# Ten instead of thirteen weight blocks converted in the first stage of an attention and feed-forward kernel, and the 1e-9 of the softmax sums kept beside them

## Chip, cores and metric

The kernel runs on one core of a Trainium2 chip. The metric is the device time of one execution in microseconds, the median of several runs.

## What is computed

Windowed attention (4 batches, 8 heads, 576 positions, head size 64; each position sees itself and the 63 before it), and behind it two feed-forward parts over all 2304 tokens. q, k and v are 32-bit floats; the weights are 64-bit floats, which arrive as pairs of 32-bit words.

```python
scores = scale * q @ k.T;  scores = where(0 <= i - j < 64, scores, -1e9)
attn = exp(scores - max);  attn = attn / (sum(attn) + 1e-9)
x = (attn @ v)                                   # 2304 x 512
x = ((x @ w1) * (x @ w2)) @ w3 @ w_out           # 512 -> 1024 -> 1024 -> 512
h = x @ w_in;  out = (h * sigmoid(h)) @ w_out2   # 512 -> 2048 -> 512
```

## The kernel before

**Stages.** Stage W (`phase_w`, 16 steps s of two parts) multiplies w3 and w_out into one matrix w' (eight blocks `wp`), so that the first feed-forward part needs one product less. Six blocks of 384 tokens then pass through `phase_a`: 16 units of 12 matmuls (L510) form a = x w1 and b = x w2 for eight slices f, their product p (L518), and eight more units multiply p by w' and store x2. The last stage (from L665) does the second feed-forward part. Attention is woven through stage W and the first five passes of `phase_a`.

**Attention.** There are 72 groups g (128 queries of one pair of heads), each with an even and an odd half, 2g and 2g + 1, in `half`. The even half has on PE the scores s of g, the output o of g - 2 and the transposes t of g - 1; on DVE the masked scores with their row minimum (L276); on ACT the copy of the transposes (L315 for the first 17, "plain" groups) and the exponentials, which write their row sums by accum_out (L287). The odd half has `normalise` on DVE (L295 adds 1e-9 to the sums, L297 takes the reciprocal, L299 multiplies), ACT's copy of o to xr (L339), and for g + 2 from group 17 on `prep_qk`: ACT rounds q and k to qkhi (L241), POOL (klo, L245) and DVE (L248) form what rounding left. Then SP loads q and k of up to g + 4; a load waits until its buffer (two of them) has been read. The first 17 groups load q to a tile of its own, qp. Half 28 + n goes out ahead of unit n of the first projection, so that o and t of two groups stand between each second pair of units.

**Conversions.** A weight block (128 x 512 values, 512 KB) passes through a line of 40 blocks and four closing steps; the counter t in `steps_to` is the step. At step t SP loads block t if `loads_to` has not done so, DVE does block t - 1's fraction and sign (`stage1`: L125, L128) and POOL adds (L132); for the 16 blocks of w1 and w2, ACT then forms the rounded part of block t - 3 (L140) and DVE or POOL the remainder of block t - 4, the low half (L144): DVE if t is even, POOL if it is odd. Last, ACT begins block t (`stage0`: L114, L115; both wait for its load).

**What sets the order.** The order on each engine is the order in which the code is written. `W12_BY` says how many of the 16 blocks of w1 and w2 (numbered here 0 to 15 in the order of their use: 0 to 3 in unit 0, 4 to 7 in unit 1, 8 to 11 in unit 8, 12 to 15 in unit 9) stand in the line by each s. `ready[s]` is the number of steps by which s has its data. In stage W each s runs to `ready[s + 2]` and loads three blocks further:

```python
loads_to(ready[s + 2] + (3 if s > 1 else 0))
steps_to(first + (ready[s + 2] - first) * (part + 1) // 2, (nc.vector, nc.gpsimd), 3)
```

The last `ready` is W12_B + 24 (L444). What is left of the line goes with the units of the first projection (the hook in L552).

Of the kernel before, what the change touches and what calls it, by code (L numbers as in the profile page):

```python
# [9 lines left out]
F32 = mybir.dt.float32  # L10
# [3 lines left out]
AF = mybir.ActivationFunctionType  # L14
ALU = mybir.AluOpType
# [12 lines left out]
MASKED = -8.0e9  # L28
PLAIN = 17
CVB, CVR = 5, 3  # L30
W12_A, W12_B = 3, 13
W12_BY = [n * W12_A // 8 for n in range(8)] + [W12_A + n * (W12_B - W12_A) // 8 for n in range(8)]


# [8 lines left out]
def tile_window_attention_ffn(ctx, tc, qkv, vp, mask, ident, w1, w2, w3t, w_out, w_in, w_out2, out):  # L43
# [7 lines left out]
    nc = tc.nc  # L51
# [4 lines left out]
    att = late.enter_context(tc.tile_pool(name="att", bufs=2, side="right"))  # L56
    psa = late.enter_context(tc.tile_pool(name="psa", bufs=1, space=PSUM))

    def f32(ap):
        return ap.bitcast(F32)  # L60
# [7 lines left out]
    def slot(name, tag, dims, dtype=F32, pool=None, bufs=1):  # L68

        t = (pool or main).tile([128, SLOTS.get(tag, 1024)], dtype, name=name, tag=tag, bufs=bufs)  # L70
        n = int(np.prod(dims))
        letters = "abcd"[: len(dims)]
        sizes = {x: d for x, d in zip(letters[1:], dims[1:])}
        return t[:, :n].rearrange(f"p ({' '.join(letters)}) -> p {' '.join(letters)}", **sizes)

    def split(hi, lo, src, eng_hi, eng_lo):

        if eng_hi == "act":
            nc.scalar.copy(out=hi, in_=src)  # L79
        else:  # L80
            (nc.vector if eng_hi == "dve" else nc.gpsimd).tensor_copy(hi, src)
        (nc.vector if eng_lo == "dve" else nc.gpsimd).tensor_tensor(  # L82
            out=lo, in0=src, in1=f32(hi), op=ALU.subtract
        )
# [4 lines left out]
    def accumulator(name, shape):  # L89

        turn[0] = (turn[0] + 1) % converting["banks"]
        return ps.tile(shape, F32, name=name, tag=f"ps{turn[0]}")
# [59 lines left out]
    def loads_to(n):  # L152
        while done["load"] < min(n, len(line)):
            if line[done["load"]]:
                line[done["load"]].load()
            done["load"] += 1
# [3 lines left out]
    def fill(n=1):  # L160

        for _ in range(min(n, len(parts))):
            parts.pop(0)()

    def steps_to(n, lo=(nc.vector,), keep=0):

        while done["step"] < min(n, len(line)):
            t = done["step"]
            loads_to(t + 1)
            fill(len(parts))  # L170
            if t >= 1 and line[t - 1]:
                parts.extend(line[t - 1].stage1())
            fill(len(parts) - keep)
            if t >= 4 and line[t - 4]:
                line[t - 4].low_part(lo[t % len(lo)])
            if t >= 3 and line[t - 3]:
                line[t - 3].high_part()
            if line[t]:
                line[t].stage0()
            done["step"] += 1  # L180
# [9 lines left out]
    qk_raw, v_raw, qk_st, v_st, s_st, p_st = {}, {}, {}, {}, {}, {}  # L190
# [3 lines left out]
    k_lo = [att.tile([128, 384], F32R, name=f"klo{i}", tag=f"klo{i}", bufs=1) for i in range(2)]  # L194
    k_p = [att.tile([128, 384], F32, name=f"kp{i}", tag=f"kp{i}", bufs=1) for i in range(2)]
    v_p = [att.tile([128, 320], F32, name=f"vp{i}", tag=f"vp{i}", bufs=1) for i in range(3)]
    HEADS = (0, slice(0, 64)), (1, slice(64, 128))
    xhl = {}
    loaded = set()
# [2 lines left out]
    def plain(g):  # L202


        return g < PLAIN

    def place(g):
        blk, r = divmod(g, 3 * NPAIR)
        return blk * 3 + r % 3, r // 3

    def load_qk(g):
        if g < NG and g not in loaded:
            loaded.add(g)
            u, c = place(g)
            if not plain(g):
                qk_raw[g] = att.tile([128, 768], F32, name=f"qk{g}", tag="qk", bufs=2)
                nc.sync.dma_start(out=qk_raw[g], in_=qkv[u, c, :, 0:768])
                return
            qk_raw[g] = att.tile([128, 128], F32, name=f"qp{g}", tag="qp", bufs=2)
            nc.sync.dma_start(out=qk_raw[g], in_=qkv[u, c, :, 0:128])  # L220

            for h, hs in HEADS:
                n = slice(384 + h * 192, 576 + h * 192)
                nc.sync.dma_start(out=k_p[g % 2][hs, h * 192 : h * 192 + 192], in_=qkv[u, c, hs, n])
# [11 lines left out]
    def prep_qk(g):  # L236
# [5 lines left out]
        q, k = slice(128, 384), slice(384, 768)  # L242
        for h, hs in HEADS:
            n = slice(384 + h * 192, 576 + h * 192)
# [38 lines left out]
    def exps(g):  # L283
        nm, rs = s_st[g]
        for h in range(2):
            x = sm[g % 2][:, h, :]
            nc.scalar.activation(  # L287
                out=x, in_=x, func=AF.Exp, scale=-1.0, bias=nm[:, h : h + 1], accum_out=rs[:, h : h + 1]
            )

    def normalise(g):
        _, rs = s_st.pop(g)
        x = sm[g % 2]
        fill()
        nc.vector.tensor_scalar_add(rs, rs, 1.0e-9)  # L295
        fill()
        nc.vector.reciprocal(out=rs, in_=rs)  # L297
        fill()
        nc.vector.tensor_tensor(out=x, in0=x, in1=rs.unsqueeze(2).to_broadcast([128, 2, 192]), op=ALU.mult)  # L299
# [12 lines left out]
    def split_t(g, t_ps):  # L312
# [6 lines left out]
        nc.scalar.copy(out=b[:, :, 0, :], in_=own)  # L319
        for h, hs in HEADS:  # L320
            nc.scalar.copy(out=a[hs, h, 0], in_=before[hs])
        nc.vector.tensor_tensor(out=b[:, :, 1, :], in0=own, in1=f32(b[:, :, 0, :]), op=ALU.subtract)
        for h, hs in HEADS:
            nc.vector.tensor_tensor(out=a[hs, h, 1], in0=before[hs], in1=f32(a[hs, h, 0]), op=ALU.subtract)
# [68 lines left out]
    def halves_to(n):  # L393
        while halves[0] < min(n, LAST_HALF):
            half(halves[0])
            halves[0] += 1
# [10 lines left out]
    def phase_w():  # L407
# [38 lines left out]
        for t in k_p + [f32(t) for t in k_lo]:  # L446
            for h, hs in HEADS:
                nc.gpsimd.memset(t[hs, 192 - h * 192 : 384 - h * 192], 0.0)
# [43 lines left out]
    def phase_a(blk, hooks):  # L492
        x = xhl[blk]
        p = [slot(f"p{blk}", "p", [5, 2, NB], F32R), slot(f"q{blk}", "q", [3, 2, NB], F32R)]
        p = [p[f // 5][:, f % 5] for f in range(8)]
        a_sb = None

        def unit(n):
            halves_to(W_HALVES + 24 * blk + n + 1)
            hooks(n)  # L500

        for s in range(16):
            f, m = divmod(s, 2)
            unit(s)
            fs = slice((f % 4) * 128, (f % 4 + 1) * 128)
            acc = accumulator(f"ab{blk}_{s}", [128, NB])
            for k in range(4):
                w = weights["12", (2 * m + f // 4) * 4 + k]
                for n, (l, r) in enumerate(PASSES):
                    nc.tensor.matmul(  # L510
                        acc, lhsT=w[:, l, fs], rhs=x[k // 2][:, k % 2, r, :],
                        start=(k == 0 and n == 0), stop=(k == 3 and n == 2),
                    )
            if m == 0:
                a_sb = slot(f"a{blk}_{f}", "st", [2, NB], bufs=4)
                nc.scalar.copy(out=a_sb[:, 0], in_=acc)
            else:
                nc.vector.tensor_tensor(out=a_sb[:, 1], in0=acc, in1=a_sb[:, 0], op=ALU.mult)  # L518
                split(p[f][:, 0], p[f][:, 1], a_sb[:, 1], "act", "pool")
        for o in range(4):  # L520
            acc = accumulator(f"x2_{blk}_{o}", [128, NB])
            for f in range(8):
                if f % 4 == 0:
                    unit(16 + 2 * o + f // 4)
                    if blk + 1 < NBLK and o == 3 and f == 0:
                        split_x(blk + 1, 3)
                    if blk + 1 < NBLK and o < 3 and f == 4:
                        split_x(blk + 1, o)
                for n, (l, r) in enumerate(PASSES):
                    nc.tensor.matmul(  # L530
                        acc, lhsT=wp[f][:, l, o * 128 : (o + 1) * 128], rhs=p[f][:, r, :],
                        start=(f == 0 and n == 0), stop=(f == 7 and n == 2),
                    )
            x2 = slot(f"x2s{blk}_{o}", "st", [NB], bufs=4)
            nc.scalar.copy(out=x2, in_=acc)
            nc.scalar.dma_start(out=x2d[o, :, blk * NB : (blk + 1) * NB], in_=x2)

    def new_pt():
# [5 lines left out]
        for i in range(2):  # L544
            for h, hs in HEADS:
                nc.gpsimd.memset(f32(pt[i, 0][hs, 1 - h]), 0.0)

    with tc.manual_schedule():
        xr = slot("xr", "xr", [4, NB])
        phase_w()  # L550
        new_pt()
        phase_a(0, lambda n: steps_to(W12_B + 24 + (n + 1) * (20 - W12_B) // 6, (nc.vector, nc.gpsimd)))  # L552
        for blk in range(1, NBLK - 1):
            phase_a(blk, lambda n: None)
        late.close()
# [33 lines left out]
        for first, last in ((0, 3), (3, 7), (7, 11), (11, 16)):  # L589
# [6 lines left out]
            for key, src in chunks:  # L596
                tag = tags.pop(0)
# [68 lines left out]
        for i in range(1, len(jobs) + 1):  # L666
            if i < len(jobs):
                j, f = jobs[i]
# [93 lines left out]
```

## Time and profile before

| what | value |
|---|---|
| median of 3 runs | 869.71 us (869.51 to 870.24) |
| profiled execution | 868.85 us, span 867.1 us |
| PE busy | 847.3 us (98% of the span) |
| DVE, ACT, POOL busy | 452.3, 497.8, 445.6 us |
| granted PE clock | 1.00 over the span |
| chain that ended last | PE 86%, DVE 1%, ACT 1% |

Busy time is the time in which the engine works on an instruction; PE's is modelled from pipelined matmuls. A timeline names, for a wait, the instruction of another engine that ended it last. t16 below means the three transposes of group 16 on PE, o15 the output of group 15, qkhi17 the rounding of group 17, klo17 its remainder on POOL.

### The profile page before, as it was taken

What the parts mean: (1) busy time and instruction counts of PE and PEld (TensorE: products, weight loads), DVE (VectorE), ACT (ScalarE), POOL (GpSimd) and SP (SyncE); (2) the same over time, 40 slices, a digit from 0 to 9 for tenths busy, and PEclk for the clock granted to TensorE, in tenths of its full rate; (3) what the DMA queues carried; (4) which work ended last, traced back from release to release, by engine and by line L of the source; (5) the groups of instructions that cost most, each with busy time, mean ns of one, the idle gap of its engine ahead of it and who ended that gap; (6) DMA issues with size and microseconds to landing.
All of it is one profiled execution on the core that took longest, in us unless ns stands there. A gap on an engine that the chain in (4) does not pass through costs nothing.

```text
span 867.1 us, 13353 instructions
## 1 busy us (share of the span) xinstructions
PE 847.3 (98%) x4362; PEld 737.0 (85%) x4362; DVE 452.3 (52%) x1158; ACT 497.8 (57%) x1243; POOL 445.6 (51%) x494
## 2 busy tenths in 40 slices
PE   5999999999999999999999999999999999999998
PEld 2444799999999999999998888888888888888896
DVE  5989878778778778676465884111111111111111
ACT  6888868788788788786666774222222222222222
POOL 4768566666666666665685886223322232223222
PEclk9999999999999999999999999999999999999999
DMA  8998233323333333330687200200020002000100
GB/s 296 336 291 261 95 97 108 120 92 101 120 92 110 112 95 120 118 92 33 245 319 274 82 1 0 98 1 1 0 98 1 1 0 73 2 1 0 49 1 25
DMA packets 43204, 85.83 MB, mean 99 GB/s; under 512 B 4864, under 2 KB 22528, under 8 KB 43136
## 3 DMA queue, kind: packets, MB, share of 16 engines
q1 hardware_dynamic: 37088, 75.55, 26.8%
q10 hardware_dynamic: 6048, 9.44, 3.0%
q8 instruction: 35, 0.57, 0.3%
q14 instruction: 33, 0.27, 0.1%
HBM read 75.53 MB, written 9.44 MB: 98 GB/s over the span
## 4 chain that ended last, share of the span: by engine, by line
PE 86%; DVE 1%; ACT 1%; issue 0%; POOLq 0%; POOL 0%; ACTq 0%; DVEq 0%
PE h L633 23%; PE o L652 23%; PE ab L510 22%; PE x L530 12%; PE t L309 2%; PE o L343 2%; PE s L266 1%; PE s L270 1%; PE o L344 1%; ACT sm L287 0%; DVE rs L295 0%; DVE a L518 0%; ACT p L79 0%; DVE cv_b L128 0%; POOLq L758 0%
## 5 line engine op out<-in xcount | busy, mean ns | idle before, releaser
L82 POOL TENSOR_TENSOR g<-sg,g 128x512 fp32r<-128x512 f32 (+1 forms) x80 | 94.9, 1186 | 249.6 <-ACT g L79 235.1
L633 PE MATMUL h<-x2t,hl 128*128 128x512 f32 (+1 forms) x960 | 213.4, 371 | 0.0
L652 PE MATMUL o<-hl,g 128*128 128x512 f32 x864 | 211.2, 391 | 0.1
L639 DVE TENSOR_TENSOR sg<-h,sg 128x512 f32<-128x512 f32 (+1 forms) x80 | 51.1, 638 | 288.2 <-ACT sg L638 288.2
L633 PEld LDWEIGHTS h<-x2t,hl 128*128 128x128 f32 x960 | 169.4, 188 | 33.9
L652 PEld LDWEIGHTS o<-hl,g 128*128 128x128 f32 x864 | 160.9, 188 | 35.6 <-POOL g L82 0.5
L638 ACT ACTIVATE sg<-h 128x512 f32<-128x512 f32 (+1 forms) x80 | 44.4, 555 | 195.4 <-PE h L633 195.4
L510 PE MATMUL ab<-xa,hl 128*128 128x384 f32 x576 | 119.2, 341 | 0.0
L510 PE MATMUL ab<-xb,hl 128*128 128x384 f32 x576 | 115.4, 334 | 0.0
L510 PEld LDWEIGHTS ab<-xb,hl 128*128 128x128 f32 x576 | 101.3, 188 | 0.0
L510 PEld LDWEIGHTS ab<-xa,hl 128*128 128x128 f32 x576 | 99.2, 188 | 0.0
L132 POOL TENSOR_TENSOR cv_b<-cv_b,cv_r 128x512 int32<-128x512 int32 x48 | 73.5, 1531 | 20.9 <-DVE cv_b L128 10.0
L79 ACT CAST g<-sg 128x512 fp32r<-128x512 f32 (+1 forms) x80 | 46.3, 578 | 63.2 <-DVE sg L639 62.3
L353 POOL TENSOR_TENSOR xr<-ot 128x128 f32<-128x128 f32 x55 | 31.5, 573 | 97.6 <-DVE ot L352 61.4
L245 POOL TENSOR_TENSOR klo<-qk,qkhi 64x192 fp32r<-64x192 f32 x110 | 66.7, 607 | 8.3 <-PE ab L510 2.0
L530 PE MATMUL x<-p,wp 128*128 128x384 f32 x360 | 68.2, 340 | 0.0
L287 ACT ACTIVATE sm<-sm,nm 128x192 f32<-128x192 f32 x144 | 64.4, 449 | 4.4 <-DVE nm L276 3.1
L530 PEld LDWEIGHTS x<-p,wp 128*128 128x128 f32 x360 | 61.9, 188 | 0.1
L125 DVE TENSOR_SCALAR cv_z<-cv_b 128x512 int32<-128x512 int32 x72 | 49.4, 687 | 15.5 <-ACT cv_b L114 14.6
L114 ACT ACTIVATE cv_b<-words 128x512 f32<-128x512 f32 x72 | 48.2, 670 | 9.7 <-DMA words<-in_w_out 5.2
L128 DVE SCALAR_TENSOR_TENSOR cv_b<-words,cv_z 128x512 int32<-128x512 int32 x72 | 49.4, 686 | 3.2
L115 ACT ACTIVATE cv_r<-words 128x512 int32<-128x512 uint32 x72 | 47.6, 661 | 0.0
(80 smaller groups left out, 1254.6 us busy)
## 6 DMA issues: line engine op xcount, KB each, us to landing
qk<-in_qkv SPq DMA_DIRECT2D x55, 384.0 KB, 3.2
words<-in_w_out SPq DMA_DIRECT2D x24, 512.0 KB, 8.3
words<-in_w3t SPq DMA_DIRECT2D x16, 512.0 KB, 6.0
words<-in_w SPq DMA_DIRECT2D x16, 512.0 KB, 6.4
words<-in_w_in SPq DMA_DIRECT2D x16, 512.0 KB, 7.2
v<-in_qkv SPq DMA_DIRECT2D x55, 96.0 KB, 2.7
x2d<-x2s ACTq DMA_DIRECT2D x24, 192.0 KB, 1.9
out_x<-osb ACTq DMA_DIRECT2D x18, 256.0 KB, 2.1
```

The costliest lines, as they stand in the source:

```text
L82: (nc.vector if eng_lo == "dve" else nc.gpsimd).tensor_tensor(out=lo, in0=src, in1=f32(hi), op=ALU.subtract)
L114: nc.scalar.activation(out=f32(self.b), in_=f32(self.high), func=AF.Copy, scale=2.0**-112)
L125: nc.vector.tensor_scalar(out=self.z, in0=b, scalar1=3, scalar2=None, op0=ALU.logical_shift_left)
L128: nc.vector.scalar_tensor_tensor(out=b, in0=self.high, scalar=-0x80000000, in1=self.z, op0=ALU.bitwise_and, op1=ALU.bitwise_or)
L132: nc.gpsimd.tensor_tensor(out=x, in0=b, in1=self.r, op=ALU.add)
L245: nc.gpsimd.tensor_tensor(out=k_lo[g % 2][hs, h * 192 : h * 192 + 192], in0=t[hs, n], in1=f32(hi[hs, n]), op=ALU.subtract)
L287: nc.scalar.activation(out=x, in_=x, func=AF.Exp, scale=-1.0, bias=nm[:, h : h + 1], accum_out=rs[:, h : h + 1])
L510: nc.tensor.matmul(acc, lhsT=w[:, l, fs], rhs=x[k // 2][:, k % 2, r, :], start=(k == 0 and n == 0), stop=(k == 3 and n == 2),)
L530: nc.tensor.matmul(acc, lhsT=wp[f][:, l, o * 128 : (o + 1) * 128], rhs=p[f][:, r, :], start=(f == 0 and n == 0), stop=(f == 7 and n == 2),)
L633: nc.tensor.matmul(acc, lhsT=weights["in", f // 4, k][:, l, fs], rhs=x[:, k, r, :], start=(k == 0 and i == 0), stop=(k == 3 and i == 2),)
L639: nc.vector.tensor_tensor(out=sg, in0=acc, in1=sg, op=ALU.mult)
L652: nc.tensor.matmul(oacc[t], lhsT=g[:, l, t * 128 : (t + 1) * 128], rhs=weights["out", f][:, r, :], start=(f == 0 and i == 0), stop=(f == 1 ...
```

## The change

Three things are edited. First, `W12_B` goes from 13 to 10, so that stage W ends 34 steps into the line instead of 37 and `W12_BY` spreads seven blocks over its second half instead of ten; the hook of the first projection then runs two steps in unit 0 and one in each of units 1 to 8, where it ran one in each of units 0 to 4 and two in unit 5. Second, the exponentials write their sums into tiles of [128, 2, 2] whose second column was set to 1e-9 once, and the addition of 1e-9 becomes a reduction over the two columns. Third, q of the plain groups is loaded into the tag of qkhi instead of one of its own.

```diff
-W12_A, W12_B = 3, 13
+W12_A, W12_B = 3, 10
...
+    sums_of = [att.tile([128, 2, 2], F32, name=f"es{i}", tag=f"es{i}", bufs=1) for i in range(2)]
+    for t in sums_of:
+        nc.vector.memset(t, 1.0e-9)
...
-            qk_raw[g] = att.tile([128, 128], F32, name=f"qp{g}", tag="qp", bufs=2)
+            qk_raw[g] = att.tile([128, 768], F32, name=f"qp{g}", tag="qkhi", bufs=2)[:, 0:128]
...
-                out=x, in_=x, func=AF.Exp, scale=-1.0, bias=nm[:, h : h + 1], accum_out=rs[:, h : h + 1]
+                out=x, in_=x, func=AF.Exp, scale=-1.0, bias=nm[:, h : h + 1], accum_out=sums_of[g % 2][:, h, 0:1]
...
-        nc.vector.tensor_scalar_add(rs, rs, 1.0e-9)
+        nc.vector.tensor_reduce(out=rs, in_=sums_of[g % 2], axis=mybir.AxisListType.X, op=ALU.add)
...
-        phase_a(0, lambda n: steps_to(W12_B + 24 + (n + 1) * (20 - W12_B) // 6, (nc.vector, nc.gpsimd)))
+        phase_a(0, lambda n: steps_to(W12_B + 26 + n, (nc.vector, nc.gpsimd)))
```

Lines of the changed file are three higher than those of the kernel before from L200 on. SP's loads from the end of stage W into the first projection, before (the last two loads of words are blocks 14 and 15; qk17 and those after it are the groups with a rounded q and k):

```order
L107 DMA words_898<-in_w2 128x1024
L107 DMA words_900<-in_w2 128x1024
L220 DMA qp15_944<-in_qkv 128x128
L224 DMA kp1_77<-in_qkv 64x192 x2
L230 DMA vp2_80<-in_vp 128x320
L220 DMA qp16_1025<-in_qkv 128x128
L224 DMA kp0_76<-in_qkv 64x192 x2
L217 DMA qk17_1029<-in_qkv 128x768
L217 DMA qk18_1031<-in_qkv 128x768
L230 DMA vp0_78<-in_vp 128x320
L217 DMA qk19_1113<-in_qkv 128x768
```

and in the changed kernel (words_1054, 1094 and 1140 are blocks 13, 14 and 15; block 12's load is the last that stage W issues):

```order
L233 DMA vp2_80<-in_vp 128x320
L223 DMA qp16_1001<-in_qkv 128x128
L227 DMA kp0_76<-in_qkv 64x192 x2
L220 DMA qk17_1005<-in_qkv 128x768
L220 DMA qk18_1007<-in_qkv 128x768
L233 DMA vp0_78<-in_vp 128x320
L107 DMA words_1054<-in_w2 128x1024
L220 DMA qk19_1091<-in_qkv 128x768
L233 DMA vp1_79<-in_vp 128x320
L107 DMA words_1094<-in_w2 128x1024
L107 DMA words_1140<-in_w2 128x1024
```

Three loads of words that stood in stage W now stand in the first projection, one ahead of qk19 and two behind it and the vp after it.

ACT from group 17's rounding in unit 3 to the exponentials of group 16 and the rounded part after them, before:

```order
L241 CAST qkhi17_1108<-qk17_1029 128x768
L140 CAST hl_1121<-cv_b_1002 128x512
L79 CAST p0_977<-a0_1_1102 128x384
L315 COPY pw1_87<-t15_1149 128x320
L287 ACTIVATE sm0_72,rs16_1142<-sm0_72,nm16_1141 128x192 x2
L140 CAST hl_1157<-cv_b_1041 128x512
```

and in the changed kernel:

```order
L244 CAST qkhi17_1086<-qk17_1005 128x768
L140 CAST hl_1101<-cv_b_978 128x512
L114 ACTIVATE cv_b_1103<-words_1094 128x512
L115 ACTIVATE cv_r_1104<-words_1094 128x512
L79 CAST p0_944<-a0_1_1080 128x384
L318 COPY pw1_91<-t15_1133 128x320
L290 ACTIVATE sm0_72,es0_81<-sm0_72,nm16_1125 128x192 x2
L140 CAST hl_1147<-cv_b_1017 128x512
```

Two instructions that read block 14's words (words_1094) now stand between the rounded part of a block and the cast of p, ahead of the exponentials of group 16; block 15's (words_1140) stand behind them.

DVE from the sums of group 14 to the product L518 (L521 in the changed file) of unit 1, before (behind one pair of L125 and L128):

```order
L295 TENSOR_SCALAR rs14_982<-rs14_982 128x2
L297 RECIPROCAL rs14_982<-rs14_982 128x2
L299 TENSOR_TENSOR sm0_72<-sm0_72,rs14_982 128x384
L125 TENSOR_SCALAR cv_z_1034<-cv_b_1002 128x512
L128 SCALAR_TENSOR_TENSOR cv_b_1002<-words_847,cv_z_1034 128x512
L144 TENSOR_TENSOR hl_1000<-cv_b_879,hl_1000 128x512
```

and in the changed kernel, from the first pair after the masked scores of group 14:

```order
L125 TENSOR_SCALAR cv_z_963<-cv_b_900 128x512
L128 SCALAR_TENSOR_TENSOR cv_b_900<-words_789,cv_z_963 128x512
L144 TENSOR_TENSOR hl_898<-cv_b_804,hl_898 128x512
L125 TENSOR_SCALAR cv_z_972<-cv_b_968 128x512
L128 SCALAR_TENSOR_TENSOR cv_b_968<-words_823,cv_z_972 128x512
L298 TENSOR_REDUCE rs14_949<-es0_81 128x2
L300 RECIPROCAL rs14_949<-rs14_949 128x2
L302 TENSOR_TENSOR sm0_72<-sm0_72,rs14_949 128x384
L125 TENSOR_SCALAR cv_z_1010<-cv_b_978 128x512
L128 SCALAR_TENSOR_TENSOR cv_b_978<-words_825,cv_z_1010 128x512
```

A low half (hl_898, block 7) and a second pair now stand ahead of the sums of group 14.

## Rows read from the trace of the kernel before

**Rows 1.** The table by stretches of the span: length, busy time (and instructions) by engine, PE clock, DMA.

```profile
57.00:97.50 40.50, 37.26 (x136) 20.14 (x135) 37.62 (x82) 33.49 (x80) 32.17 (x28) 1.00 0.72 225
...
126.00:402.00 276.00, 276.00 (x1730) 275.36 (x1729) 214.16 (x717) 225.80 (x680) 174.21 (x262) 1.00 0.34 104
```

**Rows 2.** Timeline of PE, behind 57 us: start us, us, engine, line, operation [idle before <-releaser].

```profile
64.03 0.49 PE L336 MATMUL o<-pw,vp 128*128 128x128 f32 x2 [1.59 <-ACT xr L339]
...
81.90 0.49 PE L336 MATMUL o<-pw,vp 128*128 128x128 f32 x2 [0.80 <-ACT xr L339]
...
83.50 0.52 PE L309 MATMUL t<-id_sb,sm 128*128 128x128 f32 x3 [0.72 <-DVE sm L299]
...
101.85 0.81 PE L262 MATMUL s<-kp,qp 128*128 128x384 f32 x2
...
115.26 0.52 PE L309 MATMUL t<-id_sb,sm 128*128 128x128 f32 x3 [0.68 <-DVE sm L299]
...
120.82 0.50 PE L309 MATMUL t<-id_sb,sm 128*128 128x128 f32 x3
```

**Rows 3.** Timeline of DVE in the second half of stage W.

```profile
59.43 0.69 DVE L125 TENSOR_SCALAR cv_z<-cv_b 128x512 int32<-128x512 int32 x1
...
60.82 0.35 DVE L276 CUSTOM_DVE_ANT_0 sm<-s,mask_sb 128x192 f32<-128x192 f32 x1
...
85.21 1.49 DVE L144 TENSOR_TENSOR hl<-cv_b,hl 128x512 fp32r<-128x512 f32 x1
```

**Rows 4.** Lines 295, 297 and 299 by source: duration in ns, min/median/max.

```profile
L295 DVE TENSOR_SCALAR rs<-rs x72: 152/432/1140, 13.8 to 402.7; 128x2 f32<-128x2 f32 x72
L297 DVE RECIPROCAL rs<-rs x72: 150/166/168, 14.6 to 403.0; 128x2 f32<-128x2 f32 x72
L299 DVE TENSOR_TENSOR sm<-sm,rs x72: 557/558/1549, 14.8 to 403.2; 128x384 f32<-128x384 f32 x72
```

**Rows 5.** Timeline of DVE in the first projection.

```profile
102.62 0.68 DVE L144 TENSOR_TENSOR hl<-cv_b,hl 128x512 fp32r<-128x512 f32 x1
103.22 0.55 DVE L518 TENSOR_TENSOR a<-ab,a 128x384 f32<-128x384 f32 x1
...
113.19 1.14 DVE L295 TENSOR_SCALAR rs<-rs 128x2 f32<-128x2 f32 x1 [1.24 <-ACT sm L287]
...
119.54 0.56 DVE L299 TENSOR_TENSOR sm<-sm,rs 128x384 f32<-128x384 f32 x1
```

**Rows 6.** Timeline of POOL in the first projection.

```profile
108.54 1.46 POOL L245 TENSOR_TENSOR klo<-qk,qkhi 64x192 fp32r<-64x192 f32 x2
...
113.01 1.29 POOL L144 TENSOR_TENSOR hl<-cv_b,hl 128x512 fp32r<-128x512 f32 x1
```

**Rows 7.** Timeline of ACT in the first projection.

```profile
99.58 0.67 ACT L114 ACTIVATE cv_b<-words 128x512 f32<-128x512 f32 x1
...
100.72 0.46 ACT L516 COPY a<-ab 128x384 f32<-128x384 f32 x1
...
107.58 0.84 ACT L241 CAST qkhi<-qk 128x768 fp32r<-128x768 f32 x1
...
111.43 0.51 ACT L79 CAST p<-a 128x384 fp32r<-128x384 f32 x1 [2.48 <-DVE a L518]
```

**Rows 8.** Timeline of SP: the loads that it issues.

```profile
99.60 0.38 SPq L230 DMA_DIRECT2D vp<-in_vp  x1
110.02 0.33 SPq L217 DMA_DIRECT2D qk<-in_qkv  x1
110.44 0.38 SPq L230 DMA_DIRECT2D vp<-in_vp  x1
```

**Rows 9.** DMA issues at 83.3 us, in the whole span, at 110.0 us: xcount, KB, us to landing.

```profile
words<-in_w SPq DMA_DIRECT2D x1, 512.0 KB, 4.7
...
words<-in_w SPq DMA_DIRECT2D x16, 512.0 KB, 6.4
...
qk<-in_qkv SPq DMA_DIRECT2D x1, 384.0 KB, 3.0
```


## Prediction before the run

> **What bounds the kernel now.** I read the table by stretches first, because the share of PE over the span hides the stages. In [rows 1] the reader is to see two regimes: in the second half of stage W (57 to 97.5 us) DVE is busy 37.62 of 40.50 us and PE 37.26, so either can be late; from 126 to 402 us PE is busy for all of 276 us. All that the change moves lies before 126 us, so a microsecond lost or won there moves the end by as much.
>
> Next the waits of PE, in its timeline [rows 2]. Behind 57 us four are left: 1.59 and 0.80 us for ACT's copy of an attention output, 0.72 us and (in the first projection, at t16) 0.68 us for DVE's product L299. What comes late behind the first is in DVE's timeline [rows 3]: a second conversion pair, from L125 at 59.43 on, stands ahead of the mask-and-minimum L276 at 60.82, whose result the exponentials wait for.
>
> **1. Three conversions leave stage W.** The order shows it does what it says: one step fewer at s = 8, 11 and 14. At s = 8 the pair of [rows 3] goes, so L276 starts 60.82 - 59.43 = 1.39 us earlier, and with it all that led to the 1.59 us. The 0.80 and 0.72 us come behind s = 11, which loses a step too. All three together are 3.11 us. Against it: the low halves take DVE and POOL by the parity of the step, and the new numbering gives blocks 3 to 6 to DVE, which POOL did before. One on DVE takes up to 1.49 us [rows 3], of which less than half is its own. DVE loses 3 x 1.4 us of conversions in a stretch with 2.9 us of slack, so the cover mostly holds; I leave 0.5 us of stalls and take **-2.6 us**. Ends: -3.1 (all three gone) and -1.4 (only the wait that the removed pair explains).
>
> **2. The sums beside 1e-9.** L295 goes from a one-input tensor_scalar to a reduce of 2 x 2 elements; the nearest rows price it at 0.15 to 0.17 us (the shortest L295, and L297) [rows 4], so its own cost is nothing. What it can give is its waiting: 0.432 us is its median and 1.140 its longest. At 113.19 it takes 1.14 us [rows 5], and POOL's 1.29 us operation from 113.01 ends at 114.30 [rows 6], when L295 ends too: DVE stood behind POOL. L297 never does (150 to 168 ns), L299 does (up to 1549 ns) [rows 4]. So the wait either goes, 0.98 us at t16, or is met two instructions later. I take 0.5 us, inside term 4. The Trainium skill, "SBUF — State Buffer", section "Who interferes with whom", says that VectorE and GpSimd take turns on one port pair, whole instructions at a time; that a tensor_scalar can take it, a tensor_reduce on trn2 never, and that a tensor_tensor with both inputs in SBUF is held by a GpSimd read as well. By that rule, which the rows bear out, L299 inherits the wait and the edit is worth 0 here instead of 0.98; the sum would be 0.5 us higher.
>
> The two memsets of four elements run before any data has come, at some 0.17 us each. The tile that q now shares with qkhi makes ACT's conversion of group 17 wait for the scores of group 15, which PE starts at 101.85 [rows 2], over five microseconds before ACT gets there; both are nothing.
>
> **3. The first projection starts with more to do.** Unit 0 now holds two steps instead of one, and block 7's low half. On DVE that is a pair of 1.4 us and a low half of 0.68 us [rows 5] ahead of the product of unit 1, L518, which ran at 103.22 and now comes 2.1 us later, at 105.3. PE needs block 7's low half last in unit 1, which ended at 101.85 [rows 2]; on DVE two pairs, a low half and the normalisation, 4.3 us, lie between it and L518, so it is there by 101.0. ACT converts p behind L518 and had no gap from there to qkhi17 at 107.58 [rows 7], so the 2.1 us are carried: qkhi17, some 0.8 us long, ends at about 108.4 + 2.1 = 110.5. What PE loses to this at t14 and t15 is part of the next term.
>
> **4. Blocks 13, 14 and 15 are loaded late.** The loads are issued up to line 37 ahead in stage W; before, 37 + 3 = 40 was all of them, now 34 + 3 = 37. The last three are issued by SP inside units 2, 3 and 4, each just before the step that converts it. Block 13's follows the vp load issued at 99.60 [rows 8] and is needed at about 108: hidden even by 6.4 us of landing. Block 14's stands on SP behind the load of qk19, and that waits until POOL's klo17 has read the buffer. In the profile klo17 began at 108.54 for 1.46 us [rows 6], and SP issued qk19 at 110.02, vp at 110.44 [rows 8]. On ACT, block 14's first conversion follows qkhi17 and one high half directly: ACT is in order, so everything behind it waits, above all the exponentials of group 16.
>
> Price: klo17 done at 110.0 + 2.1 = 112.1; two issues, 0.9 us, so the load leaves at 113.0. Landing: a 512 KB block in a thin stream took 4.7 us, the median of the 16 is 6.4, and 384 KB alone took 3.0 [rows 9]. I take 4.7, the nearest (a small vp ahead of it there too): 117.7. ACT's pair takes 100.72 - 99.58 = 1.14 us [rows 7]: done at 118.85. There the split of p starts, which started at 111.43 before: 7.4 us later. From it to t16 it took 115.26 - 111.43 = 3.8 us, now 0.5 less. So t16 comes at 122.2: **+6.9 us**, all of it on PE, since t16 was already late by 0.68. Ends: landing in 3.0 us and L299 not held, +4.7; landing in 6.4 and L299 held, +9.1. The Trainium skill, "DMA: Bandwidth & Descriptors", section "Anatomy of one DMA", fits 2.0 us plus bytes at 436 GB/s (on the GpSimd path), an estimate of 3.2 us for a block; the rows here are above it by 1.5 us and more, and by it the sum would be 1.5 us lower.
>
> **5. The two groups behind it.** From L299 of t16 (ended 115.1) to that of t17 (119.54 + 0.56 = 120.1, [rows 5]) the chain over ACT and DVE took 5.0 us, and PE 120.82 - 115.26 = 5.56 between its own [rows 2]. Now block 15's pair stands on ACT ahead of qkhi18 (+1.1), DVE gets there sooner by most of the 0.5 us that L299 gained (+0.4), and block 15's L125 and L128 stand on DVE behind qkhi18 (+1.4): 7.9 against 5.56, **+2.3 us** (0.9, the DVE pair alone, to 2.6). One group later two high halves and a low half are extra: **+0.5 us** (0 to 1.2), the same for the low half of block 15, which unit 9 needs. Then ACT and DVE are back to the old load, and PE bounds.
>
> **Sum:** -2.6 + 6.9 + 2.3 + 0.5 = **+7.1 us**. The profiled execution took 868.85 us (span 867.1), which makes 875.95; the median of the runs lies 0.86 above it, so I forecast **876.8 us**. By the ends the forecast's own case runs from 869.7 - 3.1 + 4.7 + 0.9 + 0 = 872.2 to 869.7 - 1.4 + 9.1 + 2.6 + 1.2 = 881.2.
>
> **Rivals.**
> - *The late load is hidden, and the kernel gets faster.* Place: ACT's wait for block 14 in unit 3. It decides at about 111 us, when ACT gets there: if the block is in by then, ACT has 2.48 us of idle time behind it [rows 7] for the moved work, terms 4 and 5 vanish, and the 0.68 us of t16 go with stage W's 2.6: 869.7 - 3.3 = 866.4. For it: PE waits for none of these conversions themselves. Against it: SP would have to issue the load some five microseconds sooner, and the order puts it behind qk19. Chance 0.07.
> - *Gain and loss cancel.* The block lands in 3.0 us, L299 is not held (+4.7), all three waits of stage W go (-3.1), and the groups behind need nothing: 869.7 + 1.6 = 871.3. For it: the DMA queue is nearly empty there. Against it: three favourable ends at once. Chance 0.10.
> - *Stage W gives nothing.* DVE becomes its bound: four low halves at 1.49 us instead of 0.68 are 3.2 us, about what the conversions free. The time is then 869.7 + 9.7 = 879.4. For it: DVE's 93% in [rows 1]. Against it: POOL has fewer operations to be in the way. Chance 0.13.
>
> **How the numbers follow.** The forecast has 0.70, with 876.8 as its time. A measurement of this kernel tells about 0.2%, 1.7 us, from no change. Faster by more than that is the first rival, 0.07; within it the second and the forecast's low edge, 0.11; slower the rest, 0.82. The range leaves out the first rival and the far ends: 871.0 to 880.8.
>
> **What would show it.** Right: in the changed profile SP issues two loads of words just behind qk19; ACT idles some 5 to 7 us for DMA before a cast of words in unit 3; PE waits 6 to 8 us for ACT or DVE at half 34 (o15, t16), and 1 to 3 us at t17; the 1.59 us of stage W is gone. Wrong: ACT's wait for that block is under 2 us, or PE runs on through t16; then the first rival holds. If the waits of PE in stage W are as before, the third does. L295's successor should never take more than 0.2 us, and L299 should be longer than before where L295 waited.

## The result, and the profile after

| what | before | after |
|---|---|---|
| median of the runs | 869.65 us (869.51 to 870.24, 4 runs) | 878.94 us (877.77 to 880.48, 4 runs) |
| profiled execution | 868.85 us, span 867.1 us | 878.86 us, span 877.1 us |

The ratio is 1.0106, with a 95% interval from 1.0092 to 1.012: the change makes the kernel 9.3 us slower. 876.8 us was forecast, with a range of 871.0 to 880.8.

The table by stretches of the span, as in [rows 1], with the columns named there (us, PE, PEld, DVE, ACT, POOL, PE clock, DMA share, GB/s), after and then before:

```profile
57.00:97.50 40.50, 40.20 (x153) 23.12 (x152) 35.76 (x86) 31.84 (x81) 25.15 (x22) 1.00 0.65 202
97.50:126.00 28.50, 18.39 (x101) 16.90 (x100) 18.39 (x41) 15.68 (x38) 17.28 (x15) 0.85 0.34 112
126.00:140.00 14.00, 14.00 (x85) 14.00 (x85) 10.01 (x32) 10.80 (x35) 9.98 (x12) 0.94 0.31 102
```

```profile
97.50:126.00 28.50, 27.82 (x175) 27.18 (x173) 22.65 (x59) 21.25 (x59) 19.08 (x19) 1.00 0.30 94
```

In the second half of stage W PE rose from 37.26 to 40.20 of 40.50 us: the waits there are gone. Between 97.5 and 126 us, the first projection, PE has 18.39 us instead of 27.82, and for the first time the granted clock is below 1: 0.85 there, 0.94 up to 140 us. Its timeline (start us, us, engine, line, operation, [idle before <-releaser]; lines are three higher than in [rows 2]) shows all the waits that it lists between 57 and 140 us, and the transposes t16, t17 and t18:

```profile
73.65 0.49 PE L339 MATMUL o<-pw,vp 128*128 128x128 f32 x2 [0.29 <-ACT xr L342]
...
93.52 0.81 PE L265 MATMUL s<-kp,qp 128*128 128x384 f32 x2
...
107.17 0.49 PE L339 MATMUL o<-pw,vp 128*128 128x128 f32 x2 [0.95 <-ACT xr L342]
...
122.09 0.80 PE L339 MATMUL o<-pw,vp 128*128 128x128 f32 x2 [9.15 <-ACT xr L342]
...
123.43 0.85 PE L312 MATMUL t<-id_sb,sm 128*128 128x128 f32 x3
...
130.87 0.50 PE L312 MATMUL t<-id_sb,sm 128*128 128x128 f32 x3
...
136.13 0.49 PE L312 MATMUL t<-id_sb,sm 128*128 128x128 f32 x3
```

One wait of 9.15 us stands in the half where t16 waited 0.68 us in [rows 2]. The clock of that half is at its lower level behind the wait (1.2 instead of 2.4 GHz, 0.50 from 122 to 127 us; columns as above):

```profile
122.00:127.00 5.00, 4.91 (x19) 4.91 (x20) 3.42 (x9) 2.51 (x8) 4.13 (x5) 0.50 0.30 96
```

ACT's timeline says what the wait is:

```profile
106.99 0.85 ACT L244 CAST qkhi<-qk 128x768 fp32r<-128x768 f32 x1
107.73 0.64 ACT L140 CAST hl<-cv_b 128x512 fp32r<-128x512 f32 x1
117.07 0.66 ACT L114 ACTIVATE cv_b<-words 128x512 f32<-128x512 f32 x1 [8.71 <-DMA words<-in_w]
117.63 0.65 ACT L115 ACTIVATE cv_r<-words 128x512 int32<-128x512 uint32 x1
118.18 0.51 ACT L79 CAST p<-a 128x384 fp32r<-128x384 f32 x1
...
120.29 0.67 ACT L114 ACTIVATE cv_b<-words 128x512 f32<-128x512 f32 x1
120.85 0.66 ACT L115 ACTIVATE cv_r<-words 128x512 int32<-128x512 uint32 x1
121.41 0.47 ACT L519 COPY a<-ab 128x384 f32<-128x384 f32 x1
121.77 0.28 ACT L342 COPY xr<-o 128x128 f32<-128x128 f32 x1
```

ACT stands for 8.71 us at block 14's words. Behind it come p, the exponentials of group 16, then block 15's pair (120.29), and only then the copy of o14 (121.77) that frees the bank for o15. SP's timeline shows the issues, POOL's the operation that they waited for, and the list of DMA issues from 109 to 112 us (xcount, KB, median us to landing) how long they took:

```profile
109.46 0.33 SPq L220 DMA_DIRECT2D qk<-in_qkv  x1
109.89 0.38 SPq L233 DMA_DIRECT2D vp<-in_vp  x1
110.31 0.90 SPq L107 DMA_DIRECT2D words<-in_w  x2
```

```profile
107.93 1.50 POOL L248 TENSOR_TENSOR klo<-qk,qkhi 64x192 fp32r<-64x192 f32 x2
```

```profile
words<-in_w SPq DMA_DIRECT2D x2, 512.0 KB, 7.0
```

In DVE's timeline the product of group 16 stands 3.2 us behind ACT's pair, and lines 298 and 302 by source (ns, min/median/max) show what the edit of the sums did:

```profile
120.31 1.09 DVE L302 TENSOR_TENSOR sm<-sm,rs 128x384 f32<-128x384 f32 x1
```

```profile
L298 DVE TENSOR_REDUCE rs<-es x72: 144/157/159, 14.1 to 412.7; 128x2 f32<-128x4 f32 x72
L302 DVE TENSOR_TENSOR sm<-sm,rs x72: 557/558/1536, 15.0 to 413.1; 128x384 f32<-128x384 f32 x72
```

### The profile page after: what moved, and what is told of

Its sections match the earlier page's. It is cut to its first block, busy times and chain, and to the rows that moved or that the text cites. A ratio compares the mean times of both kernels' runs of the same rounds, so it can differ in the third digit from the quotient of the medians.

```text
span 877.1 us, 13384 instructions
## 1 busy us (share of the span) xinstructions
PE 850.0 (97%) x4362; PEld 738.1 (84%) x4362; DVE 439.9 (50%) x1163; ACT 497.7 (57%) x1243; POOL 442.8 (50%) x491
## 4 chain that ended last, share of the span: by engine, by line
PE 76%; POOL 7%; issue 4%; DMA 1%; ACT 1%; DVE 0%; POOLq 0%; SPq 0%; ACTq 0%; DVEq 0%
PE h L636 23%; PE o L655 22%; PE ab L513 15%; PE x L533 10%; POOL klo L248 2%; PE t L312 2%; POOL q L82 1%; POOL vhl L82 1%; POOL xr L356 1%; PE o L346 1%; PE s L269 1%; PE s L273 1%; DMA words<-in_w 1%; PE o L347 1%; POOL p L82 1%
## 5 line engine op out<-in xcount | busy, mean ns | idle before, releaser
L125 DVE TENSOR_SCALAR cv_z<-cv_b 128x512 int32<-128x512 int32 x72 | 49.5, 687 | 21.9 <-ACT cv_b L114 21.4
L128 DVE SCALAR_TENSOR_TENSOR cv_b<-words,cv_z 128x512 int32<-128x512 int32 x72 | 49.5, 688 | 3.1
```

Of the source, the lines that this page charges most:

```text
L125: nc.vector.tensor_scalar(out=self.z, in0=b, scalar1=3, scalar2=None, op0=ALU.logical_shift_left)
L128: nc.vector.scalar_tensor_tensor(out=b, in0=self.high, scalar=-0x80000000, in1=self.z, op0=ALU.bitwise_and, op1=ALU.bitwise_or)
```

## The experiments

The theory after this reading: blocks 14 and 15, which are loaded late, cost everything, because ACT takes its work in order; the rest of the change is a gain. Rivals: the first projection is overfull by itself; the clock that falls behind the wait is part of the price.

Single executions differ in the first 57 us (see the last section; the reason is open). So beside the medians a second measure is used: the time of the profiled execution less the start of the scores of group 8 on PE (56.55 us before: `s8`). "W" is the time from s8 to the scores of group 14, "behind" what follows them.

| kernel | median us | ratio, 95% interval | profiled us | s8 | from s8, against before | W | behind |
|---|---|---|---|---|---|---|---|
| before | 869.65 | | 868.85 | 56.55 | 0 | 39.51 | 772.79 |
| the change | 878.94 | 1.0092 to 1.012 | 878.86 | 57.46 | +9.10 | 36.06 | 785.34 |
| early loads | 870.41 | 1.0 to 1.0018 | 870.21 | 56.74 | +1.17 | 36.07 | 777.40 |
| sums alone | 867.79 | 0.9973 to 0.9993 | 867.25 | 56.72 | -1.77 | 38.42 | 772.11 |
| blocks alone | 878.27 | 1.0083 to 1.0111 | 877.33 | 57.31 | +7.72 | 36.42 | 783.60 |
| filled wait | 878.55 | 1.0085 to 1.0113 | 877.90 | 57.14 | +8.46 | 36.06 | 784.70 |
| 15 a unit later | 883.65 | 1.0155 to 1.0183 | 885.86 | 59.65 | +13.91 | 36.07 | 790.14 |
| 15 alone late | 874.9 | 1.0043 to 1.0071 | 874.86 | 59.26 | +3.30 | 36.06 | 779.54 |
| twelve, early | 866.42 | 0.9953 to 0.9978 | 865.30 | 55.95 | -2.95 | 37.24 | 772.11 |
| eleven, early | 869.34 | 0.9989 to 1.0007 | 869.50 | 57.23 | -0.03 | 37.23 | 775.04 |
| twelve, two at 13 | 866.81 | 0.9957 to 0.9981 | 866.70 | 56.89 | -2.49 | 37.49 | 772.32 |
| twelve, two at 9 | 866.87 | 0.9958 to 0.9982 | 866.53 | 57.22 | -2.99 | 36.97 | 772.34 |

### All loads early

The change, with the last three blocks loaded in stage W as before:

```diff
-            loads_to(ready[s + 2] + (3 if s > 1 else 0))
+            loads_to(ready[s + 2] + (6 if s > 12 else 3 if s > 1 else 0))
```

> The changed kernel, with the last three weight blocks loaded inside stage W again (six lines ahead instead of three from s = 13 on); conversions stay where the change put them. Theory (the late loads hold ACT, which is in order, and PE behind it): ACT's 8.7 us wait for words in unit 3 goes; o15 then waits about 2 us for ACT's copy of o14, which stands behind block 15's conversion; the clock stays at 1.00; time 868 to 871 us. Rival (the moved conversions themselves overload ACT and DVE in units 0 to 8): the time stays above 874 us.

870.41 us: the theory's range. The late loads cost 8.5 us (878.94 - 870.41), 7.93 from s8. But the change with early loads is still not faster than before: stage W is 3.44 us shorter, what follows 4.61 us longer. PE's timeline shows where:

```profile
106.44 0.49 PE L339 MATMUL o<-pw,vp 128*128 128x128 f32 x2 [0.94 <-ACT xr L342]
...
114.06 0.49 PE L339 MATMUL o<-pw,vp 128*128 128x128 f32 x2 [1.84 <-ACT xr L342]
...
120.59 0.49 PE L339 MATMUL o<-pw,vp 128*128 128x128 f32 x2 [0.76 <-ACT xr L342]
...
126.62 0.44 PE L513 MATMUL ab<-xb,hl 128*128 128x384 f32 x1 [0.78 <-POOL hl L144]
```

Four waits, 4.32 us: nine units with six blocks' conversions beside their own work are overfull, also when every block is there in time.

### The sums alone, and the blocks alone

The sums alone are the kernel before with the second and third edit of the diff; the blocks alone are the change without the second. The third edit was not run by itself.

> The kernel before with the edit on the sums alone (and q of the plain groups in the shared tile). Theory (POOL's turn is only met two instructions later, at L299's place): 869.2 to 870.2 us, the reduce takes 0.16 us each, and the product behind it is longer where L295 waited. Rival (the wait is really saved): 0.7 us and more off t16, below 869.0.

867.79 us: faster, by 1.9 us. The rival had the time (below 869.0), but not the place: it put 0.7 us and more at t16, where the 0.68 us became 0.28; stage W, which neither had named, is 1.09 us shorter. Between 57 and 97.5 us DVE's busy time by line was 3.74 us in L295 and 3.71 in L299 before (six of each); now it is (us, busy, PE clock, DMA share, GB/s; first the reduce L298, then the product L302):

```profile
57.00:97.50 40.50, 0.90 (x6) 1.00 0.73 228
```

```profile
57.00:97.50 40.50, 4.13 (x6) 1.00 0.73 228
```

2.84 us leave the first, 0.42 come back at the second: in a stage where DVE is nearly full, most of the wait is not met again. The timelines of DVE and POOL show why. In the three groups in which L295 had taken longest (0.92 to 0.93 us) a conversion instruction (L128) and the reciprocal stand between the reduce and the product, and POOL's operation ends before the product begins; of the six products one, at 81.09, meets POOL. First the products, then POOL's operations, of the first and of that one:

```profile
63.30 0.56 DVE L302 TENSOR_TENSOR sm<-sm,rs 128x384 f32<-128x384 f32 x1
...
81.09 1.35 DVE L302 TENSOR_TENSOR sm<-sm,rs 128x384 f32<-128x384 f32 x1
```

```profile
62.02 1.27 POOL L132 TENSOR_TENSOR q<-cv_b,cv_r 128x512 int32<-128x512 int32 x1
...
80.76 1.26 POOL L132 TENSOR_TENSOR cv_b<-cv_b,cv_r 128x512 int32<-128x512 int32 x1
```

> The changed kernel with the sums as before (1e-9 added by L295). Theory (the sums edit is worth nothing here): 878.9 us, within 0.8. Rival (the edit saved about 1 us in stage W and at t16): 879.9 and more.

878.27 us, within the error of the whole change. Stage W gives 3.09 us without the sums' edit, and its wait for o15 is 7.56 us. Beside the late load the edit is worth nothing that a median shows. From s8 the blocks alone are 1.38 us better than the whole change, but that is the landing in this one execution: SP issues blocks 14 and 15 together here too (110.51 us, 0.90 us for both), and they land in 5.5 us in the median instead of 7.0; block 14's conversion begins 5.21 us behind the issue, 6.76 in the change.

```profile
words<-in_w SPq DMA_DIRECT2D x2, 512.0 KB, 5.5
```

```profile
115.72 0.66 ACT L114 ACTIVATE cv_b<-words 128x512 f32<-128x512 f32 x1 [7.15 <-DMA words<-in_w]
```

Why the same two loads land 1.5 us sooner is open.

### The wait filled with work

48 matmuls (their result is read by nobody) run in the 9.15 us, so that PE does not idle; the rest is the change.

```diff
+            if g == PLAIN:
+                warm = accumulator("warm", [128, NB])
+                for i in range(48):
+                    nc.tensor.matmul(warm, lhsT=weights["12", 0][:, 0, 0:128], rhs=xhl[0][0][:, 0, 0, :], start=True, stop=True)
```

> The changed kernel with 48 additional matmuls on PE, whose result nobody reads, between s17 and o15, that is inside the 9.2 us wait (48 x 0.174 = 8.4 us). Theory (PE's clock fell to half for 5.5 us because PE stood idle): the granted clock stays at 1.00 from 94 to 140 us, the two units behind t16 take 4.2 us instead of 5.9, and the time falls by 2 to 2.7 us, to about 876.5. Rival (the clock fell for another reason, or the fill only makes o15 later): no change or slower, 878.9 us or more.

The clock stayed up, the time did not follow: 878.55 us, against 878.94 inside the error. The stretches, and PE's timeline:

```profile
97.50:126.00 28.50, 26.73 (x159) 25.18 (x158) 18.41 (x41) 15.73 (x38) 17.35 (x15) 1.00 0.34 112
126.00:140.00 14.00, 12.45 (x78) 11.88 (x77) 9.77 (x29) 10.79 (x35) 9.61 (x12) 1.00 0.35 106
```

```profile
112.46 8.49 PE L371 MATMUL warm<-xa,hl 128*128 128x384 f32 x48
121.76 0.49 PE L339 MATMUL o<-pw,vp 128*128 128x128 f32 x2 [0.81 <-ACT xr L342]
...
128.27 0.49 PE L339 MATMUL o<-pw,vp 128*128 128x128 f32 x2 [0.73 <-ACT xr L342]
...
134.31 0.44 PE L517 MATMUL ab<-xb,hl 128*128 128x384 f32 x1 [0.82 <-POOL hl L144]
```

With the clock at 1.00 the two units behind t16 run at their old pace (4.25 us from 122.73 to 126.98, 4.28 before), and the next group then waits 0.73 us for ACT and unit 9 0.82 us for block 15's low half. In the change the lower clock stands in the place of these waits: PE at half speed waits for less. Block 14's conversion begins 6.74 us behind its issue here, as in the change (6.76), so the two traces can be compared: behind the scores of group 14 the filled wait is 0.64 us shorter. That is what the clock can have cost by these two traces, and the medians do not tell it from nothing.

### Block 15 apart from block 14

First block 15's load and conversion one unit later, then block 15 alone late (14 loaded in stage W).

```diff
-        phase_a(0, lambda n: steps_to(W12_B + 26 + n, (nc.vector, nc.gpsimd)))
+        phase_a(0, lambda n: steps_to(W12_B + (29 if n == 4 else 26 + n), (nc.vector, nc.gpsimd)))
```

```diff
-            loads_to(ready[s + 2] + (3 if s > 1 else 0))
+            loads_to(ready[s + 2] + (5 if s > 12 else 3 if s > 1 else 0))
```

> Block 15's load and its pair on ACT go from unit 4 to unit 5, behind the copy of o14 to xr. Theory (o15 waits for that copy, which stood behind the pair, and the two loads that are issued together share the way): the copy comes 1.1 us earlier for the pair, and block 14 lands in 4.7 to 5.5 us instead of 6.8, another 1.3 to 2.1 us; the wait of 9.15 us at o15 falls to 6 to 7 us and the time from 878.9 to about 876 to 877. Rival A (only the load holds ACT, the pair's place is nothing): the wait falls only by what the landing gains, 877 to 878. Rival B (the groups behind take all of it back): 878.5 to 879.

Theory and both rivals missed: 883.65 us, slower than the change. ACT's timeline shows the copy and the landing where the theory had them, and what it left out:

```profile
117.59 0.66 ACT L114 ACTIVATE cv_b<-words 128x512 f32<-128x512 f32 x1 [7.04 <-DMA words<-in_w]
...
120.67 0.28 ACT L342 COPY xr<-o 128x128 f32<-128x128 f32 x1
...
128.94 0.66 ACT L114 ACTIVATE cv_b<-words 128x512 f32<-128x512 f32 x1 [6.75 <-DMA words<-in_w]
```

The load of block 14 left SP at 112.50 and landed in 5.0 us, and the copy of o14 came 3.08 us behind block 14's pair instead of 4.70. The wait at o15 fell to 5.85 us. But block 15 now left SP behind qk20, at 124.11, and ACT stood for it a second time (6.75 us); PE then waited 3.67 us for masked scores and 1.52 us for the next output. In the change ACT did not have to wait for block 15 when it came to it (120.29). That block 14 landed in 5.0 us does not show what a second load behind it costs: the blocks alone have 5.21 us with it.

> The change with blocks 13 and 14 loaded in stage W; block 15 alone is still issued behind qk19. Theory (block 14, whose pair stands ahead of the exponentials of group 16, is the whole cost): ACT gets to block 15 near 116 us, when it is in or nearly so; PE waits 2 to 3 us in all in the first projection, as with all loads early, and the time is 870 to 872. Rival (any load behind qk19 stalls ACT for most of its landing): ACT waits 3 us or more for block 15, o15 waits with it, and the time is 873 to 876.

874.9 us lies with the rival by the median, but the profiled execution (874.86 us) began 2.5 us late (s8 at 59.26, 56.74 with all loads early); where the others stood at s8 is not on record. Neither's waits came: ACT's is below the rival's 3 us, PE's above the theory's 2 to 3.

```profile
117.05 0.66 ACT L114 ACTIVATE cv_b<-words 128x512 f32<-128x512 f32 x1 [2.18 <-DMA words<-in_w]
```

From s8 block 15 alone costs 2.13 us more than none: ACT waits 2.18 us for it, o15 4.12 us instead of 1.84. Blocks 14 and 15 together cost 7.93, so by subtraction most of it is block 14, which stands ahead of the exponentials (block 14 late by itself was not run); but block 15 is not free.

### Fewer blocks moved

Eleven and twelve blocks in stage W, with all loads early and one step in each unit; the sums as in the change (for twelve; for eleven W12_B is 11 and the first 4 is 5):

```diff
-W12_A, W12_B = 3, 10
+W12_A, W12_B = 3, 12
...
-            loads_to(ready[s + 2] + (3 if s > 1 else 0))
+            loads_to(ready[s + 2] + (4 if s > 12 else 3 if s > 1 else 0))
...
-        phase_a(0, lambda n: steps_to(W12_B + 26 + n, (nc.vector, nc.gpsimd)))
+        phase_a(0, lambda n: steps_to(W12_B + 25 + n, (nc.vector, nc.gpsimd)))
```

> Twelve blocks in stage W, all loads issued there, one step of the line in each of units 0 to 7, and the sums beside 1e-9. Theory (stage W gains by the pair that leaves it, the first projection loses only by what is crowded into its first nine units): stage W gives 1 to 2.5 us, the first projection loses less than with ten (which lost 4.3 us in four waits), 866 to 868. Rival (a block fewer is worth nothing by itself, the sums' edit gives all): 867.8, as with the sums alone. Rival (the low half of the last blocks is late in unit 9): 869 to 870.

> As the run with twelve blocks, but eleven, and one step in each of units 0 to 8. Theory: between the twelve and the ten with early loads (870.4): stage W ahead by about 3 us, waits in the first projection of 2 to 4 us, 867 to 869.5. Rival (the waits come from the number of steps in units 0 to 4 and not from the number of blocks): as with twelve, within 0.5 us.

Twelve: 866.42 us, as the theory had it, 0.34% faster than before (ratio 0.9966); with its two variants below it is the fastest of this study. Eleven: 869.34, at the upper end of what the theory gave. Both shorten stage W by the same 2.3 us, of which 1.1 are the edit of the sums; with eleven what follows loses 2.25 us again, with twelve nothing. So of the 2.95 us that twelve gain from s8, 1.77 are the sums' and 1.18 the block's: the rival that gave all to the sums (867.8) is 1.4 us off by the median. PE's timeline of the kernel with twelve blocks holds two waits behind 57 us:

```profile
63.43 0.49 PE L339 MATMUL o<-pw,vp 128*128 128x128 f32 x2 [1.58 <-ACT xr L342]
...
112.01 0.52 PE L312 MATMUL t<-id_sb,sm 128*128 128x128 f32 x3 [0.31 <-DVE sm L302]
```

Its 1.58 us is the pair at s = 8, so two more kernels place the twelve otherwise, by the second half of `W12_BY` alone (`[3, 4, 5, 6, 7, 8, 9, 10]` above):

```diff
-W12_BY = [n * W12_A // 8 for n in range(8)] + [W12_A + n * (W12_B - W12_A) // 8 for n in range(8)]
+W12_BY = [n * W12_A // 8 for n in range(8)] + [3, 3, 4, 5, 6, 7, 9, 10]
```

The second has `[3, 3, 5, 6, 7, 8, 9, 10]`.

> The twelve blocks with all loads early, placed otherwise in stage W: none at s = 8, two at s = 13. Theory of term 1 (the wait of 1.59 us is the second pair ahead of the masked scores at s = 8): that wait goes, and nothing comes in its place if DVE has room at s = 13: 1 to 1.6 us less than the 866.4 of the run with twelve, 864.8 to 865.4. Rival (a pair always costs its wait somewhere): the wait turns up behind s = 13, 866 to 866.8.

> As the run before, but the pair goes from s = 8 to s = 9, which then has two. Theory of term 1: at s = 9 two pairs again stand ahead of masked scores, so a wait of 0.8 to 1.6 us takes the place of the 1.59 us: 865.6 to 866.6. Rival (only the first of the half is tight): the wait is gone, 864.8 to 865.4.

866.81 and 866.87 us: no difference to 866.42 that the runs can tell. At s = 13 the rival has it (a wait turns up behind it), at s = 9 the theory (its wait; the time is 0.3 us above its range). PE's timeline, with two at s = 13:

```profile
73.06 0.49 PE L339 MATMUL o<-pw,vp 128*128 128x128 f32 x2 [0.28 <-ACT xr L342]
...
85.82 0.49 PE L339 MATMUL o<-pw,vp 128*128 128x128 f32 x2 [0.56 <-ACT xr L342]
...
87.16 0.52 PE L312 MATMUL t<-id_sb,sm 128*128 128x128 f32 x3 [0.46 <-DVE sm L302]
```

and at s = 9:

```profile
69.15 0.49 PE L339 MATMUL o<-pw,vp 128*128 128x128 f32 x2 [1.06 <-ACT xr L342]
```

The 1.58 us is gone in both, and 1.30 and 1.06 us have come: in both placements the wait moved with the pair that makes it.

## Why the prediction was right, and where its terms were not

The sign and the mechanism held: the late load of block 14 ahead of the exponentials. The profiled execution took 878.86 us where the sum gave 875.95. Of the 2.9 us between them 0.9 are the later start of that execution, and 2.0 come from the terms as follows: +3.8 in term 4, -0.85 in term 1, and about -1 in term 5. Term 4 left its own ends, so that the total stayed well inside the range owes something to luck.

1. **Three conversions leave stage W: -2.6 forecast.** The scores of group 14 came 2.54 us earlier in the trace, but in an execution whose s8 was 0.91 us late. From s8 the whole change gave 3.45 us, the blocks alone 3.09: the forecast's far end of 3.1, all three waits. The 0.5 us left for low halves that go to DVE were not needed.
2. **The sums: worth nothing in stage W, 0.5 at t16.** At t16 it was 0.40 (the sums alone). The reduce never took over 159 ns, and the product of group 16 took 1.09 us: the wait for POOL was met at the product there, as the Trainium skill, "SBUF — State Buffer", section "Who interferes with whom", has it. What failed is that the term looked at t16 alone. L295 took 3.74 us of DVE in the second half of stage W by itself, and only 0.42 of the 2.84 us that it gave up came back, since POOL was done before five of the six products began: 1.9 us for the sums alone. In the change 0.36 us of it is left in stage W (36.06 us, 36.42 for the blocks alone), where PE is busy 40.20 of 40.50 us.
3. **DVE and ACT 2.1 us behind at unit 3.** Right: with the 2.6 us of stage W, qkhi17 was to end at 107.9; it ended at about 107.8, where ACT's next begins (107.73). klo17 ended at 109.43; 109.5 was forecast.
4. **Block 14: +6.9.** This term was too small. By its steps, all less the 2.6 us: the load was to leave at 110.4 (left from 110.31), to land by 115.1 (117.07), ACT's pair to be done at 116.25 (118.18). The landing was mis-sized: 6.8 us instead of 4.7. The price for one block was right where one went by itself (4.9, 5.0 and 4.7 us in two runs); but block 15's load stands directly behind it on SP, and the two were issued within 0.90 us. The forecast named the two loads and priced one. That they shared the way is the likely reason, but not shown: with the same two loads block 14's conversion began 6.76, 6.74 (filled wait) and 5.21 us (blocks alone) behind the issue. The row for the 16, 6.4, was the better one for this execution. From the pair to the end of the product the chain took 3.22 us (118.18 to 121.40), 3.3 forecast. Then a step was missing: t16 stands behind o15 on PE, and o15 waits for the copy of o14, which stands behind block 15's pair on ACT. That put o15 at 122.09, 0.7 us after the product, and t16 1.34 us behind it. With 1.9 us from the landing and 2.0 from this, t16 came at 123.43 instead of 119.6: the term was 10.7 us (8.17 behind [rows 2], and the 2.54 that stage W had given), beyond its far end of 9.1.
5. **The two groups behind: +2.8.** No wait stood at t17, which the forecast had named as a sign. The trace lost 1.88 us there all the same (t16 is 8.17 us behind [rows 2], t17 10.05), by the clock: unit 6 and 7 took 5.93 us instead of 4.28. The filled wait shows that the chain over ACT and DVE was there, 1.55 us in two waits, and that PE at the lower clock hides it. The size was right within a microsecond, the sign to look for was not. One group later (t18) nothing more was lost (10.02 us), where 0.5 was forecast.

Terms 4 and 5 together were +9.7 and came to about 12.6 behind the scores of group 14. Of the rivals, the hidden load fell at ACT's 8.71 us, and "gain and loss cancel" at the landing, 6.8 us instead of 3.0. "Stage W gives nothing" gave 879.4, near the result, and is refuted by the waits of stage W that are gone: a time alone would not have told it from the forecast.

## What to carry to other kernels

A load that is issued later is priced together with every load that stands behind it on the same queue, and its wait together with all that stands behind it on an engine that works in order: here two blocks of 512 KB, asked for late, cost 8 us, since the exponentials stood behind the first reader of the one and the copy that PE's next output waits for behind that of the other. Move work out of a full stage only as far as the next stage has room: beside the sums' edit, one block out was worth its 1.18 us of stage W, two shortened stage W no further and lost 2.9 us behind it, three shortened it by another 1.2 and lost 5.3 (all loads early). And when an instruction that waits for a shared resource is replaced, count its waits over the whole stage where its engine is nearly full, not at the one place where another engine shows a gap.

## What the runs showed of the hardware

- **Two transfers issued together.** A load of 512 KB by itself behind 384 KB and 96 or 160 KB took 4.7 to 5.0 us; two issued within 0.90 us took 7.0 in the median in the change and in the filled wait, but 5.5 in the blocks alone. What makes the difference is open. The Trainium skill, "DMA: Bandwidth & Descriptors", section "Anatomy of one DMA", gives a fit for the GpSimd path by which a block would take 3.2 us, an estimate; every row shown here is above it.
- **The clock after a wait.** After 9.15 us in which PE did nothing, its granted clock was at the lower of the two levels (1.2 instead of 2.4 GHz) from 122 to 127 us (0.50): t16's three transposes took 0.85 us instead of 0.52. With matmuls in the gap it stayed at 1.00. The medians show no gain from that (878.55 us, 878.94).
- **An operation that waits for POOL and one that does not.** The addition of 1e-9 by L295 took 152 to 1140 ns in [rows 4], the reduce in its place 142 to 159 ns in all 72 cases of the sums alone, where POOL's work is as before.
- **The start varies.** s8 came between 55.95 and 59.65 us in twelve profiled executions. Five kernels that are the same program up to there had it at 57.46 (the change), 56.74 (early loads), 57.14 (filled wait), 59.65 and 59.26 (the two with block 15 apart). From there to the scores of group 14 all five took 36.06 or 36.07 us. Why was not tried and stays open.
